# Raw parameters loaded in 2 KB runs, thirty-five copies placed on the other engine, one subtraction for two in a linear-attention and state-space kernel

## The chip, the cores and the metric

The kernel runs on one core of one Trainium2 chip. The core has TensorE (PE, matmuls into PSUM), VectorE (DVE), ScalarE (ACT), GpSimd (POOL, here only fills and DMA issues) and SyncE (SP, DMA issues). Each engine executes its own instructions in order; semaphores order the engines among each other. The metric is the device time of one execution in microseconds (us), as the median of several runs. The trace was taken from one further, profiled execution.

## What is computed

Two independent branches on 2048 tokens of width 448, whose bf16 results are put side by side into 896 columns. Branch A is linear attention with 16 heads of 28 and the feature map softmax(p), softmax(-p); branch B is a state-space convolution with 448 channels of 256 complex states each.

```python
# A
q, k, v = split(x @ wqkv)                       # 16 heads of 28
phi = lambda p: concat(softmax(p), softmax(-p))
phi_q, phi_k = phi(q @ w_phi), phi(k @ w_phi)
kv = einsum("bhsf,bhsd->bhfd", phi_k, v);  z = phi_k.sum(tokens)
o  = (phi_q @ kv) / (phi_q @ z + 1e-6)
a  = o @ wo
# B
dt = exp(log_dt);  P = exp(dt * (A_re + 1j*A_im) * l)        # l = 0..2047
K  = einsum("dn,dnl,dn->dl", C, P, dt*B).real
y  = irfft(rfft(u, 4096) * rfft(K, 4096))[:2048] + u * Dskip
out = concatenate([a, y], axis=-1)
```

## The kernel before

The program is recorded first: each call of a helper adds one operation to a list (`Prog.add`), some 1100 in all, and names its engine. Then the operations are issued in the order of a table of numbers, `ORDER`, written out by hand; a second table, `SLOTS`, names the PSUM bank of each job. So the order of instructions on each engine is that of the table, and the waits between engines follow from which operation reads or overwrites what. PSUM has eight banks; a bank that ScalarE and VectorE both read is read by one after the other.

The helpers are `mul`, `add`, `sub` (VectorE, line 162), `smul` (VectorE, times a constant, L174), `vcopy` (VectorE, L180), `recip` (VectorE, L187), `af` (ScalarE function, L190), `acopy` (copy on ScalarE, L193), `mms` and `transposes` (TensorE, L201 and L211), `dma` (L216, from SP or POOL). A copy that changes f32 to bf16 is named CAST in the trace.

The stages, by the names of the functions:

- Raw parameters: six arrays of 448x256 bf16 (A, B, C, real and imaginary) are loaded, 224 KB each. `to_states` multiplies them by diagonal matrices DG of dt, which also brings states to the partitions: 128 states (two halves of 256) by 896 columns of channels. `log_dt` is loaded as [4, 112], put through exp and turned on TensorE into [112, 4] in PSUM. For A, ScalarE copies the result from PSUM to bf16 (the high part), and VectorE subtracts that from PSUM (the low part); ScalarE exponentials read the same banks. From A come powers (`amp`, `cs`, PW) by products, from B and C the coefficients CR. `ones` matmuls over CR give K0.
- `flip_x` transposes x on TensorE; a copy brings it back to SBUF. `fold_weights` multiplies the key and query weights with w_phi. `signal_spectrum(b)`, b = 0, 1: sums and differences of u, matmuls with a table G1, and eight copies of 128x896 from PSUM, then a store to SUd in DRAM.
- `key_side`: eight pairs of token blocks. For a pair: projections on TensorE, four exponentials and two copies of V on ScalarE, one DMA transpose by SP (L600) into the one buffer ET, 14 matmuls of ET with a constant HZ (the sums of the softmax), a reciprocal on VectorE (L187), a product VR on VectorE, 16 matmuls that add to the key-value sums. HZ lies in SBUF where `ones` lay before.
- For a quarter `qt` of the channels: `rotations` and `dampings` (sines and exponentials on ScalarE), `damp`, `far`, `hi_tables` (products on VectorE, the largest 128x6720), `build_k` (small matmuls and copies), `scatter_k` (through DRAM), then kernel spectrum and `conv` (products of 3584, sums, inverse matmuls, store). `query_side(sc)`, sc = 0 to 3, stands between them.

The operations of the four quarters, the two signals, the pairs of keys and the query blocks are interleaved by ORDER.

Of the kernel before, what the change touches and what calls it, by code (L numbers as in the profile page):

```python
# [46 lines left out]
def _dft_tables():  # L47
# [6 lines left out]
    GI = np.stack([GO, GO[:, :, :, ::-1]])  # L54
    e = _round_bf16(np.arange(2048)).astype(np.int64)
# [27 lines left out]
class Prog:  # L83
# [10 lines left out]
    def add(self, eng, fn):  # L94
        self.ops.append((eng, fn))

    def issue(self, i):
        self.ops[i][1]()
# [7 lines left out]
def kernel(  # L106
# [57 lines left out]
    def mul(o, a, b):  # L164
        tt(o, a, b, ALU.mult)
# [4 lines left out]
    def sub(o, a, b):  # L170
        tt(o, a, b, ALU.subtract)

    def smul(o, a, s):
        prog.add("V", lambda: nc.vector.tensor_scalar_mul(o, a, s))  # L174
# [4 lines left out]
    def vcopy(o, a):  # L179
        prog.add("V", lambda: nc.vector.tensor_copy(o, a))  # L180
# [11 lines left out]
    def acopy(o, a):  # L192
        prog.add("A", lambda: nc.scalar.copy(o, a))  # L193
# [60 lines left out]
    ldt = sb(oSQ + 2816, [4, 112])  # L254
    dtr = sb(oSQ + 3072, [4, 112])

    def load_raw(nm):
        dma("S", raw[nm], srcs[nm].rearrange("(j p) n -> p j n", p=112))
# [5 lines left out]
    dma("S", ldt, bass.AP(tensor=B_log_dt.tensor, offset=B_log_dt.offset, ap=[[112, 4], [1, 112]]))  # L264
# [38 lines left out]
    (b_,) = prog.take("P", 6)  # L303
    dtp = bank16(b_, [112, 4])
    transposes([(dtp, dtr, PID[0:4, 0, 0:4])])
    mul(DG, PID[0:112, 0, 0:112].unsqueeze(1).to_broadcast([112, 4, 112]), dtp.unsqueeze(2).to_broadcast([112, 4, 112]))
# [38 lines left out]
    for part, terms in enumerate(([("CreBre", DG), ("CimBim", DGN)], [("CreBim", DG), ("CimBre", DG)])):  # L345
# [141 lines left out]
    def damp(qt, x0, w):  # L487
        A = amps(qt)
        smul(W[:, 1, 0:31:2, x0:x0 + w], A[:, 0:31:2, x0:x0 + w], -1.0)
        for part in (1, 0):  # L490
            for r, n, d, tr in ((0, 15, QC, 0), (30, 1, 0, 15)):
                o = W[:, part, r, x0:x0 + 1]
                a, step = A[:, r, x0:x0 + 1], d
                if part:
                    step = A[:, r + d // QC, x0:x0 + 1].offset - o.offset
                    a = o
                b = T[:, part, tr, x0:x0 + 1]
                if n > 1:
                    mul(view(o, [2 * QC, n], [d, 2], [1, w]), view(a, [2 * QC, n], [step, 2], [1, w]),
                        view(b, [QC, n], [0, 2], [1, w]))  # L500
                else:
                    mul(view(o, [1, w]), view(a, [1, w]), view(b, [1, w]))
# [53 lines left out]
    def build_k(qt, c):  # L556
        for hq in range(2):
# [12 lines left out]
            x0 = 14 * c + 7 * hq  # L570
            acopy(TS[qt % 2][:, :, x0:x0 + 7], psum[:, b, 0:7 * N_LO].rearrange("p (c l) -> p l c", c=7))
# [178 lines left out]
    def conv(qt, SU, UD, S_, OB, banks):  # L750
# [7 lines left out]
        def finish(b, t):  # L758
# [5 lines left out]
            sub(S[:, 1, 0], y[:, 0, 0:448], y[:, 0, 448:896])  # L764
            sub(S[:, 1, 1], y[:, 1, 448:896], y[:, 1, 0:448])
# [156 lines left out]
```

## Time and profile before

| | |
|---|---|
| median of 3 runs | 302.82 us (300.65 to 304.51) |
| profiled execution | 301.71 us, span 299.6 us |
| granted TensorE clock, mean | 0.949 |
| busy: TensorE, VectorE, ScalarE, POOL | 240.7, 244.4, 203.4, 16.0 us |
| VectorE idle before its last key reciprocal (114.89 us) | 40.6 us |
| VectorE idle from there to its last instruction (292.90 us) | 8.0 us |

The span runs from the first to the last instruction of the trace; the profiled execution's time is 2.1 us longer than it. "Busy" is time in which at least one instruction of the engine runs; instructions overlap a little in the pipeline, so that the sum of their durations is somewhat larger. A wait is put down to what released it.

### The profile page before, as it was taken

To read this page: it belongs to the slowest core of one execution; us is meant where nothing else is said; L and a number is where in the kernel's file an instruction comes from. 1 tells how busy PE (TensorE), PEld (TensorE's weight loads), DVE (VectorE), ACT (ScalarE), POOL (GpSimd) and SP (SyncE) were. 2 spreads that over 40 slices of the span, in tenths; PEclk is the share of its full clock that TensorE was granted. 3 is DMA by queue.
4 is the path that set the end of the run, shared out by engine and by line. 5 is a ranking of instruction groups with operands and counts; after the bars stand their busy time and mean duration, and the time that the engine had idled before them with its cause. 6 is when DMAs were issued, how large, how long until landed. Compare 5 with 4: busy or idle time off the path is not lost. (4 is left out here: it accounts for less than half of the span.)

```text
span 299.6 us, 8829 instructions
## 1 busy us (share of the span) xinstructions
PE 240.7 (80%) x3877; PEld 179.8 (60%) x3877; DVE 244.4 (82%) x292; ACT 203.4 (68%) x343; POOL 16.0 (5%) x32
## 2 busy tenths in 40 slices
PE   1246997899469999986979996566998888999784
PEld 1245554567245567863447763466658678999784
DVE  4265995446249999997989999989899999999991
ACT  3749999599947999997199955871948611544431
POOL 8102201001000000000000001000000000000000
PEclk9999999999959999998695999777999999999999
DMA  7999387463804530045012533955879956667222
GB/s 161 239 231 194 79 246 145 64 181 67 107 10 122 122 64 4 6 136 104 3 61 58 85 79 85 331 146 109 227 255 293 301 136 176 147 184 135 46 65 63
DMA packets 65966, 39.47 MB, mean 132 GB/s; under 512 B 46616, under 2 KB 61992, under 8 KB 65544
## 3 DMA queue, kind: packets, MB, share of 16 engines
q1 hardware_dynamic: 62920, 31.57, 45.0%
q0 software_dynamic: 3008, 7.34, 8.9%
q8 instruction: 30, 0.49, 0.7%
q14 instruction: 8, 0.07, 0.1%
HBM read 26.36 MB, written 8.85 MB: 118 GB/s over the span
## 5 line engine op out<-in xcount | busy, mean ns | idle before, releaser
L201 PE MATMUL psum<-sbuf 128*16 128x48 bf16 (+9 forms) x3768 | 231.3, 258 | 39.1 <-DVE sbuf L162 11.1
L201 PEld LDWEIGHTS <-sbuf 128*16 128x16 bf16 (+4 forms) x3768 | 170.7, 109 | 98.3 <-issue 37.3
L162 DVE TENSOR_TENSOR sbuf<-sbuf 128x896 bf16<-128x896 bf16 (+13 forms) x227 | 216.7, 1002 | 12.1 <-DMA sbuf<-SCd 3.5
L193 ACT CAST sbuf<-psum 128x448 bf16<-128x448 f32 (+4 forms) x141 | 74.9, 581 | 70.6 <-PE psum L201 63.1
L190 ACT ACTIVATE sbuf<-psum 128x448 bf16<-128x448 f32 (+4 forms) x140 | 81.7, 674 | 13.2 <-DVE sbuf L162 7.5
L211 PE MATMUL psum<-sbuf 128*112 128x128 bf16 (+3 forms) x109 | 11.7, 267 | 16.2 <-DMA sbuf<-in_A_x_dram 7.2
L190 ACT ACTIVATE sbuf<-psum,sbuf 128x896 bf16<-128x896 f32 (+3 forms) x28 | 21.7, 812 | 0.0
L211 PEld LDWEIGHTS <-sbuf 128*112 128x112 bf16 (+3 forms) x109 | 10.0, 172 | 17.8 <-DMA sbuf<-in_A_x_dram 7.7
L187 DVE RECIPROCAL sbuf<-psum 128x64 bf16<-128x64 f32 x8 | 4.4, 555 | 19.4 <-PE psum L201 19.4
L190 ACT ACT_TABLE_LOAD x13 | 16.7, 1283 | 0.9 <-PEq L906 0.7
L190 ACT ACTIVATE sbuf<-sbuf 128x896 bf16<-128x896 bf16 (+3 forms) x13 | 11.6, 915 | 3.6 <-DVE sbuf L162 3.4
L180 DVE COPY sbuf<-psum 112x1024 bf16<-112x1024 bf16 (+2 forms) x16 | 7.3, 466 | 7.8 <-PE psum L211 6.6
L216 POOL DMA_DIRECT2D sbuf<-const x4 | 2.2, 556 | 126.0 <-PE psum L201 109.5
L162 DVE TENSOR_TENSOR sbuf<-psum,sbuf 128x128 f32<-128x128 f32 (+3 forms) x10 | 4.7, 491 | 3.8 <-ACT sbuf L193 3.8
L193 ACT COPY sbuf<-psum 112x896 bf16<-112x896 bf16 x5 | 4.5, 919 | 4.7 <-PE psum L211 4.7
L216 POOL DMA_DIRECT2D sbuf<-in_B_u_dram x8 | 6.6, 830 | 19.0 <-DMA sbuf<-in_B_B_re_dram 18.9
L174 DVE TENSOR_SCALAR sbuf<-sbuf 128x3584 bf16<-128x3584 bf16 (+4 forms) x11 | 6.5, 587 | 0.0
L216 POOL DMA_DIRECT2D sbuf<-SUd x4 | 2.1, 529 | 72.5 <-DVE sbuf L162 72.5
L193 ACT CAST sbuf<-sbuf 128x1792 bf16<-128x1792 f32 x3 | 5.1, 1703 | 0.0
L180 DVE COPY sbuf<-sbuf 128x448 bf16<-128x448 bf16 (+1 forms) x6 | 1.4, 238 | 3.1 <-DMA sbuf<-const 3.1
L177 DVE SCALAR_TENSOR_TENSOR sbuf<-sbuf 128x64 f32<-128x64 f32 (+1 forms) x6 | 3.0, 506 | 0.0
L196 POOL MEMSET sbuf<- 128x32 bf16 (+3 forms) x6 | 1.4, 261 | 24.7 <-PE psum L211 24.5
(12 smaller groups left out, 9.4 us busy)
## 6 DMA issues: line engine op xcount, KB each, us to landing
sbuf<-const SPq DMA_DIRECT2D x16, 384.0 KB, 3.2
SUd<-sbuf SPq DMA_DIRECT2D x8, 448.0 KB, 4.3
sbuf<-SCd SPq DMA_DIRECT2D x16, 224.0 KB
sbuf<-SUd POOLq DMA_DIRECT2D x4, 896.0 KB, 4.9
sbuf<-const POOLq DMA_DIRECT2D x2, 1024.0 KB, 7.9
sbuf<-in_A_x_dram SPq DMA_DIRECT2D x4, 448.0 KB
out_dram<-sbuf SPq DMA_DIRECT2D x4, 448.0 KB
sbuf<-in_B_u_dram SPq DMA_DIRECT2D x16, 112.0 KB, 4.0
```

The lines of the kernel that those rows point to most:

```text
L162: prog.add("V", lambda: nc.vector.tensor_tensor(out=o, in0=a, in1=b, op=op))
L174: prog.add("V", lambda: nc.vector.tensor_scalar_mul(o, a, s))
L177: prog.add("V", lambda: nc.vector.scalar_tensor_tensor(out=o, in0=a, scalar=s, in1=b, op0=op0, op1=op1))
L180: prog.add("V", lambda: nc.vector.tensor_copy(o, a))
L187: prog.add("V", lambda: low(lambda: nc.vector.reciprocal(o, a)))
L190: prog.add("A", lambda: nc.scalar.activation(o, a, fn, **kw))
L193: prog.add("A", lambda: nc.scalar.copy(o, a))
L196: prog.add("G", lambda: nc.gpsimd.memset(o, v))
L201: nc.tensor.matmul(o, lhsT=l, rhs=r, **kw)
L211: nc.tensor.transpose(o, i, idn)
L216: prog.add(eng, lambda: e.dma_start(out=o, in_=i))
```

## The change

1. Raw parameters are loaded as "(p j) n" instead of "(j p) n": partition p holds channels 4p to 4p+3, one run of 2 KB, instead of four runs of 512 B from channels p, 112+p and so on. `log_dt` comes as [112, 4] in the same manner, so that its transpose on TensorE, and the bank for it, fall away. The order of columns that the later stages expect is restored in `to_states`, whose matmuls have 56 columns instead of 112 and are twice as many (48 to 96), in the K0 matmuls (8 to 16), and in the column steps of the copy to TS in `build_k`.
2. `Prog.add` takes a second form of an operation, for the other engine. 35 operations, listed in OTHER, are issued in that form. 18 go from ScalarE to VectorE: nine copies of 128x896 f32 from PSUM (the high part of A, real and imaginary, one half of CR, six of signal_spectrum), one of 112x896 f32 and three of 112x896 bf16 in fold_weights, three of 448 columns f32 from PSUM (K0, one V of keys, one of the query side), two casts of 128x1792 f32 in SBUF (two powers). 17 go from VectorE to ScalarE: two copies of flip_x, two tiny ones for KVZ, four of 128x128 f32 and four of 128x128 bf16 in query_side, two of 448 in hi_tables(2) and (3), and three multiplications by a constant (one of 3584 in damp(2), two of 448 in far(3)).
3. In `conv`, the two subtractions of 448 become one of 896; the sign goes into the table GI.
4. `damp` writes its parts in another order; the count and size of its operations stay.
5. ORDER and SLOTS are new.

```diff
+    GI[1, :, 1] *= -1
...
-    def add(self, eng, fn):
-        self.ops.append((eng, fn))
+    def add(self, eng, fn, other=None):
+        self.ops.append((eng, fn, other))
 
     def issue(self, i):
-        self.ops[i][1]()
+        eng, fn, other = self.ops[i]
+        (other if i in OTHER else fn)()
...
     def smul(o, a, s):
-        prog.add("V", lambda: nc.vector.tensor_scalar_mul(o, a, s))
+        prog.add("V", lambda: nc.vector.tensor_scalar_mul(o, a, s), lambda: nc.scalar.activation(o, a, ACT.Copy, scale=s))
...
     def vcopy(o, a):
-        prog.add("V", lambda: nc.vector.tensor_copy(o, a))
+        prog.add("V", lambda: nc.vector.tensor_copy(o, a), lambda: nc.scalar.copy(o, a))
...
     def acopy(o, a):
-        prog.add("A", lambda: nc.scalar.copy(o, a))
+        prog.add("A", lambda: nc.scalar.copy(o, a), lambda: nc.vector.tensor_copy(o, a))
...
     def load_raw(nm):
-        dma("S", raw[nm], srcs[nm].rearrange("(j p) n -> p j n", p=112))
+        dma("S", raw[nm], srcs[nm].rearrange("(p j) n -> p j n", j=4))
...
-    dma("S", ldt, bass.AP(tensor=B_log_dt.tensor, offset=B_log_dt.offset, ap=[[112, 4], [1, 112]]))
+    dma("S", ldt, bass.AP(tensor=B_log_dt.tensor, offset=B_log_dt.offset, ap=[[4, 112], [1, 4]]))
...
     af(dtr, ldt, ACT.Exp)
-    (b_,) = prog.take("P", 6)
-    dtp = bank16(b_, [112, 4])
-    transposes([(dtp, dtr, PID[0:4, 0, 0:4])])
-    mul(DG, PID[0:112, 0, 0:112].unsqueeze(1).to_broadcast([112, 4, 112]), dtp.unsqueeze(2).to_broadcast([112, 4, 112]))
+    mul(DG, PID[0:112, 0, 0:112].unsqueeze(1).to_broadcast([112, 4, 112]), dtr.unsqueeze(2).to_broadcast([112, 4, 112]))
...
         for j in range(4):
             for nch in range(2):
-                at = (j % 2) * QC + nch * 56
-                o = view(psum[:, bs[j // 2], at:at + 1], [112, 2], [14, 4], [1, 14])
-                items += acc(o, [(t[:, j, 128 * nch:128 * nch + 128],
-                                  d[:, j, :].rearrange("p (g c q) -> p c g q", c=2, q=14)) for t, d in terms])
+                for h in range(2):
+                    at = 112 * (j // 2) + 56 * nch + 7 * (j % 2)
+                    o = view(psum[:, bs[h], at:at + 1], [QC, 2], [14, 4], [1, 7])
+                    items += acc(o, [(t[:, j, 128 * nch:128 * nch + 128],
+                                      d[:, j, 56 * h:56 * h + 56].rearrange("p (a g r) -> p a g r", a=2, r=7))
+                                     for t, d in terms])
...
             add(S[:, 0], y[:, :, 0:448], y[:, :, 448:896])
-            sub(S[:, 1, 0], y[:, 0, 0:448], y[:, 0, 448:896])
-            sub(S[:, 1, 1], y[:, 1, 448:896], y[:, 1, 0:448])
+            sub(S[:, 1], y[:, :, 0:448], y[:, :, 448:896])
...
+OTHER = {int(i) for i in (
+    "33 36 49 52 56 73 94 98 102 104 110 112 115 130 132 152 155 157 232 330 333 445 453 499 507 588 625 633 644 "
+    "666 674 706 768 902 936 "
+).split()}
```

Three places show how the new order moves instructions. Lines of the changed kernel are numbered two or three higher (L164 for L162, L195 for L193, L189 for L187).

VectorE, from the start, after its three fills. Before, the first four operations are DG, the low part of A's real part, DGN and a copy of flip_x:

```order
L162 TENSOR_TENSOR sbuf<-sbuf,psum 112x448
L162 TENSOR_TENSOR sbuf<-psum,sbuf 128x896
L174 TENSOR_SCALAR sbuf<-sbuf 112x448
L180 COPY sbuf<-psum 112x2x4x128
L180 COPY sbuf<-sbuf 112x16
L180 COPY sbuf<-psum 112x2x4x128 x2
```

Now, with the copies of the high parts (CAST 128x896) and the three bf16 copies of fold_weights (COPY 112x896) between them:

```order
L164 TENSOR_TENSOR sbuf<-sbuf 112x448
L176 TENSOR_SCALAR sbuf<-sbuf 112x448
L195 CAST sbuf<-psum 128x896
L164 TENSOR_TENSOR sbuf<-psum,sbuf 128x896
L195 CAST sbuf<-psum 128x896
L164 TENSOR_TENSOR sbuf<-psum,sbuf 128x896
L164 TENSOR_TENSOR sbuf<-sbuf 112x1024 x4
L164 TENSOR_TENSOR sbuf<-sbuf 128x1792
L182 COPY sbuf<-psum 112x2x4x128
L164 TENSOR_TENSOR sbuf<-sbuf 128x1792
L195 COPY sbuf<-psum 112x896
L182 COPY sbuf<-psum 112x2x4x128
```

Both pairs of copy and subtraction are on VectorE, and the four products of raw parameters (112x1024) follow directly.

VectorE, in the key stage. Before, from the fifth reciprocal to behind the sixth; the products of 6720 are damp(0), those of 3584 and 2x1792 far(0):

```order
L187 RECIPROCAL sbuf<-psum 128x64
L162 TENSOR_TENSOR sbuf<-sbuf 128x1856
L174 TENSOR_SCALAR sbuf<-sbuf 128x16x224
L162 TENSOR_TENSOR sbuf<-sbuf 128x6720
L162 TENSOR_TENSOR sbuf<-sbuf 128x224
L162 TENSOR_TENSOR sbuf<-sbuf 128x6720
L162 TENSOR_TENSOR sbuf<-sbuf 128x224
L162 TENSOR_TENSOR sbuf<-sbuf 128x2x1792
L162 TENSOR_TENSOR sbuf<-sbuf 128x3584
L162 TENSOR_TENSOR sbuf<-sbuf 128x1792
L187 RECIPROCAL sbuf<-psum 128x64
```

Now, from the second reciprocal to the fourth:

```order
L189 RECIPROCAL sbuf<-psum 128x64
L164 TENSOR_TENSOR sbuf<-sbuf 128x1856
L164 TENSOR_TENSOR sbuf<-sbuf 128x3584
L164 TENSOR_TENSOR sbuf<-sbuf 128x4x224
L164 TENSOR_TENSOR sbuf<-sbuf 128x224
L164 TENSOR_TENSOR sbuf<-sbuf 128x4x224
L164 TENSOR_TENSOR sbuf<-sbuf 128x6720
L189 RECIPROCAL sbuf<-psum 128x64
L164 TENSOR_TENSOR sbuf<-sbuf 128x1856
L164 TENSOR_TENSOR sbuf<-sbuf 128x3584
L164 TENSOR_TENSOR sbuf<-sbuf 128x6720
L189 RECIPROCAL sbuf<-psum 128x64
```

The two products of 6720 stand in two different gaps between reciprocals, three pairs earlier.

ScalarE, between the powers of A and the copies of the first signal. Before, the big exponential (128x1792) is followed by copies of fold_weights and of the signal (128x2x4x112), and by the sines of A:

```order
L190 ACTIVATE sbuf<-sbuf 128x1792
L193 CAST sbuf<-psum 112x896
L190 ACTIVATE sbuf<-psum,sbuf 128x896
L190 ACTIVATE sbuf<-psum 128x896
L193 CAST sbuf<-psum 112x896
L190 ACTIVATE sbuf<-psum,sbuf 128x896
L193 CAST sbuf<-sbuf 128x1792
L193 CAST sbuf<-psum 128x2x4x112 x2
```

Now, from the same operation on; the functions on 128x224 and 128x2x224, and those of 128x896 after them, are rotations(0):

```order
L192 ACTIVATE sbuf<-sbuf 128x1792
L195 CAST sbuf<-psum 128x896
L192 ACTIVATE sbuf<-psum 128x896
L192 ACTIVATE sbuf<-psum,sbuf 128x224
L192 ACTIVATE sbuf<-psum 128x224
L195 CAST sbuf<-psum 112x896
L192 ACTIVATE sbuf<-psum 128x2x224
L192 ACTIVATE sbuf<-psum,sbuf 128x896
L195 CAST sbuf<-psum 112x896
L192 ACTIVATE sbuf<-psum 128x224
```

The cast of a power and the signal's copies have left this place, and rotations(0) fill it; before, these stood behind the fifth pair's exponentials.

## Rows read from the trace of the kernel before

**Rows 1.** The page, part 1: busy us (share of the span) and instructions
```profile
PE 240.7 (80%) x3877; PEld 179.8 (60%) x3877; DVE 244.4 (82%) x292; ACT 203.4 (68%) x343; POOL 16.0 (5%) x32
```

**Rows 2.** Windows: length, busy of each engine, clock, DMA share, GB/s
```profile
0.00:10.00 10.00, 1.15 (x9) 0.85 (x9) 4.07 (x6) 4.10 (x5) 7.17 (x15) 1.00 0.80 190
10.00:53.88 43.88, 30.72 (x240) 20.59 (x241) 29.15 (x37) 37.23 (x48) 4.45 (x8) 1.00 0.81 178
53.88:114.89 61.01, 53.38 (x478) 33.89 (x480) 41.12 (x41) 51.80 (x85) 1.25 (x3) 0.94 0.46 91
114.89:292.90 178.01, 152.29 (x3096) 121.48 (x3097) 170.04 (x212) 109.23 (x204) 3.18 (x6) 0.93 0.50 134
292.90:299.60 6.70, 3.13 (x64) 2.97 (x61) 0.00 (x0) 1.06 (x2) 0.00 (x0) 1.00 0.31 67
```

**Rows 3.** VectorE's longest wait: us in total, times, longest
```profile
DVE sbuf L187 <- PE psum L201: 19.4, 5, 8.4
```

**Rows 4.** VectorE's timeline: start, us, line, operation, [idle before <-releaser]
```profile
53.88 0.56 DVE L187 RECIPROCAL sbuf<-psum 128x64 bf16<-128x64 f32 x1 [4.70 <-PE psum L201]
...
74.53 0.55 DVE L187 RECIPROCAL sbuf<-psum 128x64 bf16<-128x64 f32 x1
...
85.22 0.56 DVE L187 RECIPROCAL sbuf<-psum 128x64 bf16<-128x64 f32 x1 [8.38 <-PE psum L201]
...
89.12 12.79 DVE L162 TENSOR_TENSOR sbuf<-sbuf 128x6720 bf16<-128x6720 bf16 x7
101.83 0.55 DVE L187 RECIPROCAL sbuf<-psum 128x64 bf16<-128x64 f32 x1
...
114.89 0.56 DVE L187 RECIPROCAL sbuf<-psum 128x64 bf16<-128x64 f32 x1 [0.43 <-PE psum L201]
```

**Rows 5.** VectorE's groups by form: busy us, mean ns of one, idle before
```profile
L162 DVE TENSOR_TENSOR sbuf<-sbuf 128x896 bf16<-128x896 bf16 x58 | 34.6, 619 | 0.9
...
L162 DVE TENSOR_TENSOR sbuf<-sbuf 128x448 bf16<-128x448 bf16 x32 | 11.3, 384 | 0.2
...
L162 DVE TENSOR_TENSOR sbuf<-sbuf 128x1792 bf16<-128x1792 f32 x3 | 6.0, 2015 | 0.0
L180 DVE COPY sbuf<-psum 112x1024 bf16<-112x1024 bf16 x8 | 5.3, 678 | 6.0 <-PE psum L211 6.0
...
L174 DVE TENSOR_SCALAR sbuf<-sbuf 128x3584 bf16<-128x3584 bf16 x3 | 3.3, 1085 | 0.0
...
L162 DVE TENSOR_TENSOR sbuf<-psum,sbuf 128x896 bf16<-128x896 f32 x2 | 2.2, 1087 | 3.8 <-ACT sbuf L193 3.8
...
L162 DVE TENSOR_TENSOR sbuf<-psum,sbuf 112x448 bf16<-112x448 f32 x2 | 1.2, 620 | 0.0
...
L180 DVE COPY sbuf<-psum 128x128 f32<-128x128 f32 x4 | 1.1, 287 | 1.2 <-PE psum L201 1.1
```

**Rows 6.** ScalarE's groups by form, the large copy from PSUM
```profile
L193 ACT CAST sbuf<-psum 128x896 bf16<-128x896 f32 x20 | 18.2, 934 | 7.7 <-PE psum L201 7.5
```

**Rows 7.** Timeline, columns as in rows 4: HZ on POOL, its matmuls, wo, the fifth pair
```profile
48.01 0.58 POOL L216 DMA_DIRECT2D sbuf<-const  x1 [16.53 <-issue]
...
53.27 2.90 PE L201 MATMUL psum<-sbuf 128*128 128x32 bf16 x26 [2.90 <-DMA sbuf<-const]
...
74.38 0.75 POOL L216 DMA_DIRECT2D sbuf<-in_A_wo_dram  x1 [0.15 <-issue]
...
84.62 7.37 PE L201 MATMUL psum<-sbuf 128*128 128x32 bf16 x50 [3.26 <-DMA sbuf<-sbuf]
```

**Rows 8.** Timeline, columns as in rows 4: the matmuls behind VectorE's last operation
```profile
292.32 3.71 PE L201 MATMUL psum<-sbuf 128*128 128x112 bf16 x72 [1.04 <-DVE sbuf L162]
```

More of the change, by code (lines that the diff above doesn't have):

```diff
@@ L253 @@
     DGN = sb(oSQ + 1920, [112, 4, 112])
-    ldt = sb(oSQ + 2816, [4, 112])
-    dtr = sb(oSQ + 3072, [4, 112])
+    ldt = sb(oSQ + 2816, [112, 4])
+    dtr = sb(oSQ + 2824, [112, 4])
     def load_raw(nm):
-        dma("S", raw[nm], srcs[nm].rearrange("(j p) n -> p j n", p=112))
+        dma("S", raw[nm], srcs[nm].rearrange("(p j) n -> p j n", j=4))
     def load_x(i):
@@ L351 @@
     bs = prog.take("P", 0)
-    mms([it for qt in range(4) for it in acc(
-        view(psum[:, bs[0], 112 * qt:112 * qt + 1], [28, 4], [14, 2], [1, 14]),
-        [(ones, view(CR[:, 0, QC * qt + 56 * nch:QC * qt + 56 * nch + 1], [14, 4], [112, 2], [1, 14]))
+    mms([it for qt in range(4) for c in range(2) for it in acc(
+        view(psum[:, bs[0], 112 * qt + 2 * c:112 * qt + 2 * c + 1], [28, 4], [1, 2], [4, 7]),
+        [(ones, view(CR[:, 0, QC * qt + 112 * c + 56 * nch:QC * qt + 112 * c + 56 * nch + 1], [14, 4], [7, 2], [1, 7]))
          for nch in range(2)])])
@@ L488, in damp, with rows_of @@
         A = amps(qt)
[L489 to L502, printed above, removed]
+        inside = qt in (0, 3)
+        def rows_of(part, a, step):
+            mul(view(W[:, part, 0, x0:x0 + 1], [2 * QC, 15], [QC, 2], [1, w]),
+                view(a[:, 0, x0:x0 + 1], [2 * QC, 15], [step, 2], [1, w]),
+                view(T[:, part, 0, x0:x0 + 1], [QC, 15], [0, 2], [1, w]))
+            mul(W[:, part, 30, x0:x0 + w], a[:, 30, x0:x0 + w], T[:, part, 15, x0:x0 + w])
+        if not inside:
+            rows_of(0, A, QC)
+        N_ = W[:, 1] if inside else A
+        smul(N_[:, 0:31:2, x0:x0 + w], A[:, 0:31:2, x0:x0 + w], -1.0)
+        rows_of(1, N_, QC - WS if inside else QC)
+        if inside:
+            rows_of(0, A, QC)
     def tmp(i):
@@ L569, in build_k @@
                 mms(items)
-            x0 = 14 * c + 7 * hq
-            acopy(TS[qt % 2][:, :, x0:x0 + 7], psum[:, b, 0:7 * N_LO].rearrange("p (c l) -> p l c", c=7))
+            acopy(TS[qt % 2][:, :, 2 * c + hq:28:4], psum[:, b, 0:7 * N_LO].rearrange("p (c l) -> p l c", c=7))
     def scatter_k(qt):
```

92 rows, old and new, of tables (ORDER, SLOTS) are left out of this document.

## Prediction, made before the changed kernel was run

> **What bounds the kernel now.** I read the page's busy shares first. VectorE is busy for 244.4 us of the 299.6, TensorE for 240.7, ScalarE for 203.4 [rows 1]. Two engines at 80% or more, each waiting for the other in turn: the averages don't say which sets the end, so the stretches come next.
>
> The windows cut the run at the first and the last of the eight reciprocals of the key stage [rows 2]. From the last one (114.89) to VectorE's last instruction (292.90) VectorE is busy 170.04 of 178.01 us: 8.0 idle. This stretch is as long as VectorE's work in it. Before 114.89 VectorE is busy 4.07 + 29.15 + 41.12 = 74.3 us, so it idles 40.6. Behind 292.90 comes a tail of 6.7 us: 72 matmuls in 3.71 us [rows 8], an eviction, a store.
>
> So the end is: time of the last key reciprocal + VectorE's work behind it + 8.0 + tail. Work taken from VectorE late is worth its full length. Work given to VectorE early is free as long as it falls into the 40.6 us.
>
> What makes the 40.6? The waits put 19.4 us of it to reciprocals that wait for TensorE, the longest 8.4 [rows 3]. In VectorE's timeline the reciprocals start at 53.88, three steps later at 74.53 (6.9 us a step), then at 85.22, 101.83 and, two steps later, 114.89 [rows 4]. Three places lose time. The first reciprocal: TensorE sits 2.90 us until 53.27 for a constant, HZ, whose load POOL issued only at 48.01 [rows 7]. HZ lies where the matrix `ones` was, so it waits for the K0 matmuls, which stand late. The fifth: TensorE waits 3.26 us for a DMA transpose, beside which ran the load of `wo`, issued at 74.38 [rows 7]. That step took 10.7 us, 3.8 over the 6.9. The sixth: 12.79 us of VectorE in one piece from 89.12, damp(0) and what follows it, stand ahead of the reciprocal at 101.83 [rows 4].
>
> **VectorE's sum.** 18 copies come from ScalarE. Ten read 128x896 or 112x896 f32 from PSUM. No copy of that form stands on VectorE; the nearest row is the subtraction with one such operand, 1.087 [rows 5]. Neighbours overlap a little in the pipeline, so I take 1.05: 10.5 us. The lower bound is the bf16 copy of 112x1024, 0.678, cut to 896 elements: 0.6 each, 6 us. Three bf16 copies of 112x896 at 0.59: 1.8. Three of 448 f32 from PSUM, nearest row 0.620 [rows 5], at 0.58: 1.7. Two casts of 1792 f32 in SBUF lie, by the nearest rows, between 0.678 (the bf16 copy) and 2.015 (a product of 1792 with an f32 operand) [rows 5]; the first is the less like it, so I take a little over the middle, 1.5: 3.0. Together 17.0, bounds 11 and 19.
>
> By the row for the same f32 copy on ScalarE, 0.934 [rows 6], the ten are about 1.2 us dearer on VectorE in all. The Trainium skill ("VectorE: DVE Perf Modes", Specifications) says the same in words, that ScalarE sits closer to PSUM. Its tier table and errata formula speak of the two SBUF casts: a one-source f32 operation may run at double rate there, an estimated 0.99 us each, by which the sum would be 1.0 lower; no row here shows it.
>
> 17 operations go to ScalarE: two flip copies at 0.678, one scaling of 3584 at 1.085, and fourteen small ones, none over the 0.287 of the 128x128 copy [rows 5], at 0.25: 5.9, less overlap 5.3. The convolution's two subtractions of 448 become one of 896, eight times: 8 x (2 x 0.384 - 0.619) = 1.2 [rows 5]. New sum: 244.4 + 17.0 - 5.3 - 1.2 = 254.9.
>
> Of the 18, only one copy of 448 (query side) stands behind the last key reciprocal; of the 17, the scaling and twelve small ones do (3.7 with overlap). Work behind it: 170.0 + 0.6 - 3.7 - 1.2 = 165.7. Work up to it: 254.9 - 165.7 = 89.2.
>
> **First reciprocal.** Ahead of it VectorE had 33.2 us. By the new order 13 of the copies come in ahead: seven f32 at 1.05, three at 0.59, one at 0.58, two at 1.5, 12.7 together. Steps of hi_tables(0) (about 2.0 by their forms), one flip copy and two tiny copies go behind it or away. That leaves 43. At the start VectorE still idles: the states of A_re wait for their load, and ScalarE's exponentials read the same banks. Before, it was busy 4.07 of the first 10 us [rows 2], some 6 idle; the second pair of banks now costs about 2 more: 8. So VectorE is there at 51. K0's copy now stands behind some 25 us of VectorE's work, and its matmuls ahead of that, so HZ's load goes out well before 48 and no longer holds TensorE. I take 51.
>
> **To the last reciprocal.** Seven steps, each the longer of 6.9 (transpose, matmuls, reciprocal, product, matmuls) and VectorE's work in it. The order now spreads damp(0) and far(0) over the steps; by the forms VectorE's work in them is 6.4, 8.6, 7.2, 5.8, 6.5, 6.8 and 5.1. That gives 8.6 + 7.2 + 5 x 6.9 = 50.3. It can be spread because the rotations of table 0, which stood on ScalarE between the exponentials of the fifth and the sixth pair, now stand ahead of all key exponentials. The load of `wo` still goes beside some transpose; between 0 and the 3.8 seen I take 1.5. Last reciprocal: 51 + 50.3 + 1.5 = 102.8, against 114.9. Idle up to there: 102.8 - 89.2 = 13.6 instead of 40.6.
>
> **End.** 102.8 + 165.7 + 8.0 = 276.5. Tail 6.7 less 0.5, since VectorE's last operation is now an addition and half of the 72 matmuls need only the subtraction ahead of it: 6.2. Span 282.7. The profiled run took 301.71 with a span of 299.6, so 2.1 lie around it: 284.8, which is 16.9 less. The median of the runs shown, 302.82, stands 1.1 above the profiled one; I forecast 285.
>
> **Costed at nothing.** The 2 KB runs for raw parameters: one load, A_re, stands on the way at the start; the others land while VectorE has other work. Bounds: 1 us gained there, or 1 lost, because x now follows all six raw loads. The 56 more matmuls (48 for the states, 8 for K0): TensorE did 240 in 30.72 us there [rows 2], 0.13 each, 7 together. It is busy 32 of the first 54 us, and this idle hides them; without it the first reciprocal would be up to 7 later. ScalarE loses about 17 and gains about 7; it idles 96 in all.
>
> **Rivals.** (1) The key loop keeps its pace. The loss would not lie in VectorE's order but in the one ET buffer, which a transpose may overwrite only when TensorE has read it, and in what TensorE does in between. Then 61.0 us pass from first to last reciprocal as before: from 51, 112.0 + 165.7 + 8.0 + 6.2 + 2.1 = 294.0; from 53.9, 296.9. For it: even with undisturbed transposes a step took 6.9, and VectorE waited. Against: the two long steps (10.7 and 16.6) have other causes with names, above.
>
> (2) Slower: in the first 51 us TensorE's banks are emptied by VectorE, in order. A copy that stands behind a 2-us product whose operand is late keeps its bank, and TensorE's next matmuls, those of the keys included, wait. To reach 308.9 (2% slower; about 2% is what a measurement of this kernel can tell from no change) the last reciprocal must come at 126.9, 24.1 later than forecast: 1.9 us lost for each of the 13 copies. Two each give 311. Against: ScalarE, which emptied these banks, was itself busy 37.23 of 43.88 us there, VectorE only 29.15 [rows 2].
>
> (3) Denser: VectorE hardly waits after the start. 8 + 89.2 = 97.2, then 165.7 + 3 + 6.2 + 2.1 = 274.2. The steps' sum of 50.3 speaks against it.
>
> (4) The placement doesn't do what it says: each copy moved to VectorE displaces VectorE's own work, and the idle stays at 40.6. 89.2 + 40.6 + 165.7 + 8.0 + 6.2 + 2.1 = 311.8. The waits would have to be set from outside both engines, as by the loads. Half of it (idle at 27) gives 298.
>
> **Chances.** Forecast 0.52 (279 to 290 for it alone); rival 1 0.25, two thirds of it under 296.8; denser 0.10; half of rival 4, 297 to 308, 0.08; rivals 2 and 4 whole 0.05. Faster by over 2%: 0.52 + 0.16 + 0.10 = 0.78; within 2%: 0.17; slower: 0.05. The range 276 to 298 leaves out half of the denser case, most of the half of rival 4 and the slower ones: 0.17.
>
> **What would show it.** VectorE's busy time near 255 and ScalarE's near 193; the first reciprocal near 51 and the last near 103; VectorE's idle before the last near 14; an f32 PSUM copy of 896 on VectorE near 1.05, the SBUF cast near 1.5; HZ issued well before 48. The forecast is wrong if the first reciprocal starts later than 54, or if the steps stay above 8 us: then look at whom TensorE waits for in the first 50 us, and at how long the transposes take.

## The result, and the profile after

The changed kernel took 287.74 us as the median of four runs (286.73 to 292.33), the kernel before 303.66 beside it. The ratio is 0.950, with an interval of 0.939 to 0.960. Two later comparisons with other runs of the kernel before gave 0.953 (0.944 to 0.963) and 0.951 (0.945 to 0.957). The forecast was 285 within 276 to 298. The profiled execution took 286.73 us with a span of 284.6, against 301.71 and 299.6 before.

The page's first part after the change (columns as in [rows 1]):

```profile
PE 236.7 (83%) x3932; PEld 179.9 (63%) x3932; DVE 255.6 (90%) x285; ACT 202.2 (71%) x340; POOL 16.1 (6%) x32
```

VectorE does 11.2 us more than before in a run that is 15 us shorter. The windows, cut at the first and the last key reciprocal and at VectorE's last instruction (columns as in [rows 2]):

```profile
0.00:10.00 10.00, 1.04 (x16) 0.88 (x16) 3.65 (x6) 5.18 (x7) 6.64 (x15) 1.00 0.82 176
10.00:52.32 42.32, 34.16 (x333) 24.84 (x334) 38.45 (x41) 34.87 (x47) 6.25 (x11) 1.00 0.73 175
52.32:99.03 46.71, 45.43 (x425) 28.64 (x423) 45.87 (x47) 40.52 (x73) 0.00 (x0) 1.00 0.55 121
99.03:277.70 178.67, 152.85 (x3101) 122.44 (x3100) 167.64 (x193) 120.61 (x214) 3.17 (x6) 0.95 0.51 136
277.70:284.60 6.90, 3.22 (x66) 3.06 (x63) 0.00 (x0) 1.06 (x2) 0.00 (x0) 1.00 0.29 63
```

Up to the last reciprocal VectorE is now busy 3.65 + 38.45 + 45.87 = 88.0 of 99.0 us: 11.1 idle where it was 40.6. Between the first and the last reciprocal it idles 0.8 us of 46.7, before 19.9 of 61.0. The last reciprocal comes 15.9 us earlier. Behind it the stretch is as long as before, 178.7 us: VectorE works 2.4 us less there, and idles 11.0 instead of 8.0. So the whole gain lies ahead of the last key reciprocal. TensorE has less to do between the two reciprocals as well: 425 matmuls and 45.4 us where it had 478 and 53.4 [rows 2]. It is recorded busy 97% of that stretch now, VectorE 98%.

VectorE's timeline at the reciprocals (start, us, line, operation, idle before where there was any; beside [rows 4]):

```profile
52.32 0.56 DVE L189 RECIPROCAL sbuf<-psum 128x64 bf16<-128x64 f32 x1
...
58.72 0.55 DVE L189 RECIPROCAL sbuf<-psum 128x64 bf16<-128x64 f32 x1
59.38 8.01 DVE L164 TENSOR_TENSOR sbuf<-sbuf 128x1856 bf16<-128x1856 bf16 x6
67.31 0.55 DVE L189 RECIPROCAL sbuf<-psum 128x64 bf16<-128x64 f32 x1
...
94.06 0.55 DVE L189 RECIPROCAL sbuf<-psum 128x64 bf16<-128x64 f32 x1
...
99.03 0.55 DVE L189 RECIPROCAL sbuf<-psum 128x64 bf16<-128x64 f32 x1
```

No reciprocal has a wait in brackets any more; the 19.4 us of [rows 3] are gone. The steps are 6.4, 8.6, 7.2, 5.9, 6.7, 6.9 and 5.0 us. The load of HZ goes out at 30.61 and that of `wo` at 50.97, ahead of the second transpose (issued at 52.30); a transpose is hardly waited for any more (0.2 us, once) (POOL's timeline):

```profile
30.61 0.57 POOL L218 DMA_DIRECT2D sbuf<-const  x1 [1.82 <-PE psum L203]
...
50.97 0.75 POOL L218 DMA_DIRECT2D sbuf<-in_A_wo_dram  x1 [0.29 <-ACT sbuf L192]
```

What the moved operations cost on their new engine (groups by form: busy us, mean ns of one, idle before):

```profile
L195 DVE CAST sbuf<-psum 128x896 bf16<-128x896 f32 x9 | 9.6, 1081 | 7.6 <-ACT sbuf L192 5.7 <-PE psum L203 1.9
...
L195 DVE CAST sbuf<-sbuf 128x1792 bf16<-128x1792 f32 x2 | 2.2, 1085 | 0.0
```

and on ScalarE, with the copies to TS of `build_k`, whose written columns the change spreads:

```profile
L195 ACT CAST sbuf<-psum 128x336 bf16<-128x336 f32 x16 | 14.3, 994 | 10.6 <-PE psum L203 10.6
...
L176 ACT ACTIVATE sbuf<-sbuf 128x3584 bf16<-128x3584 bf16 x1 | 3.2, 3190 | 0.1
...
L182 ACT COPY sbuf<-psum 112x1024 bf16<-112x1024 bf16 x2 | 2.1, 1044 | 0.0
```

### The profile page after: what moved, and what is told of

It reads as the page before. It is cut to its first block, busy times and chain, and to the rows that moved or that the text cites. A ratio compares the mean times of both kernels' runs of the same rounds, so it can differ in the third digit from the quotient of the medians.

```text
span 284.6 us, 8940 instructions
## 1 busy us (share of the span) xinstructions
PE 236.7 (83%) x3932; PEld 179.9 (63%) x3932; DVE 255.6 (90%) x285; ACT 202.2 (71%) x340; POOL 16.1 (6%) x32
## 4 chain that ended last, share of the span: by engine, by line
DVE 36%; PE 32%; DMA 15%; issue 7%; ACT 5%; SPq 3%; POOL 1%; DVEq 0%; POOLq 0%
DVE sbuf L164 33%; PE psum L203 31%; DMA sbuf<-SCd 7%; DMA sbuf<-in_A_x_dram 5%; ACT sbuf L192 3%; SPq L218 3%; ACT sbuf L195 2%; DMA SCd<-sbuf 1%; DVE sbuf L189 1%; DVE sbuf L176 1%; DMA out_dram<-sbuf 1%; DMA sbuf<-in_B_u_dram 1%; PE psum L213 1%; POOL sbuf L218 1%; ACT L192 0%
## 5 line engine op out<-in xcount | busy, mean ns | idle before, releaser
L203 PE MATMUL psum<-sbuf 128*16 128x48 bf16 (+10 forms) x3824 | 229.0, 256 | 36.0 <-DVE sbuf L164 10.5
L164 DVE TENSOR_TENSOR sbuf<-sbuf 128x896 bf16<-128x896 bf16 (+13 forms) x220 | 217.2, 1033 | 10.4 <-PE psum L203 3.5
L195 ACT CAST sbuf<-psum 128x448 bf16<-128x448 f32 (+4 forms) x128 | 70.9, 605 | 55.7 <-PE psum L203 54.1
L192 ACT ACTIVATE sbuf<-psum 128x448 bf16<-128x448 f32 (+4 forms) x140 | 83.9, 668 | 9.9 <-PE psum L203 9.7
L195 DVE CAST sbuf<-psum 128x896 bf16<-128x896 f32 (+2 forms) x13 | 12.4, 974 | 7.7 <-ACT sbuf L192 5.7
L213 PE MATMUL psum<-sbuf 128*112 128x128 bf16 (+2 forms) x108 | 10.3, 259 | 8.2 <-DVE sbuf L164 7.0
L213 PEld LDWEIGHTS <-sbuf 128*112 128x112 bf16 (+2 forms) x108 | 9.1, 165 | 9.8 <-DMA sbuf<-in_A_x_dram 5.5
L192 ACT ACTIVATE sbuf<-sbuf 128x896 bf16<-128x896 bf16 (+3 forms) x13 | 11.8, 905 | 4.6 <-DVE sbuf L164 3.9
L176 DVE TENSOR_SCALAR sbuf<-sbuf 128x896 bf16<-128x896 bf16 (+3 forms) x8 | 4.9, 609 | 1.7 <-ACT sbuf L192 1.5
L182 ACT COPY sbuf<-psum 128x128 f32<-128x128 f32 (+2 forms) x10 | 4.3, 427 | 2.6 <-PE psum L213 2.1
L164 DVE TENSOR_TENSOR sbuf<-psum,sbuf 128x128 f32<-128x128 f32 (+3 forms) x10 | 4.7, 492 | 0.5 <-ACT sbuf L182 0.4
L176 ACT ACTIVATE sbuf<-sbuf 128x448 bf16<-128x448 bf16 (+1 forms) x3 | 4.4, 1455 | 0.9 <-DVE sbuf L164 0.9
L189 DVE RECIPROCAL sbuf<-psum 128x64 bf16<-128x64 f32 x8 | 4.4, 550 | 0.1
L182 DVE COPY sbuf<-psum 112x1024 bf16<-112x1024 bf16 x6 | 4.1, 684 | 0.3 <-PE psum L213 0.2
```

What stands on the lines that cost most here:

```text
L164: prog.add("V", lambda: nc.vector.tensor_tensor(out=o, in0=a, in1=b, op=op))
L176: prog.add("V", lambda: nc.vector.tensor_scalar_mul(o, a, s), lambda: nc.scalar.activation(o, a, ACT.Copy, scale=s))
L182: prog.add("V", lambda: nc.vector.tensor_copy(o, a), lambda: nc.scalar.copy(o, a))
L189: prog.add("V", lambda: low(lambda: nc.vector.reciprocal(o, a)))
L192: prog.add("A", lambda: nc.scalar.activation(o, a, fn, **kw))
L195: prog.add("A", lambda: nc.scalar.copy(o, a), lambda: nc.vector.tensor_copy(o, a))
```

## Experiments

All ratios are to the kernel before on the same chip. The changed kernel itself ran again beside HZ, wo and the four copies (0.953, 286.52 us), and beside the second run of the raw parameters, the TS copies and the two operations (0.951, 285.49 us). The other runs are compared with it by these ratios.

A time in a trace can differ between executions. In the six traces whose operations ahead of the first reciprocal are those of the changed kernel, that reciprocal starts between 51.90 and 54.00 us.

**The order without the placement.** The changed kernel, all 35 operations on their old engines:

```diff
-OTHER = {33, 36, 49, 52, 56, 73, ... 936}
+OTHER = set()
```

> The changed kernel with all 35 operations back on their old engines; order, banks and loads of the changed kernel stay. Theory (the end is the last key reciprocal plus VectorE's work behind it, and the placement fills VectorE's idle time of the first 50 us while ScalarE is relieved there): VectorE's work behind the last reciprocal grows by about 3.1 us, and ScalarE, busy 40 of the first 52 us, takes 13 copies of 0.6 to 1.7 us back, 12 us, so that it sets the pace there: first reciprocal at 57 to 60 instead of 52.3, time 295 to 299. Rival (the new order alone carries the gain, the placement only swaps one busy engine for another): first reciprocal within 1 us of 52.3, time 290 to 292.

304.16 us, 1.014 of the kernel before (1.0005 to 1.028). The four times were 300.36, 303.24, 305.08 and once 658.53 us, which no trace explains and which lifts the median; so no gain is shown, rather than a loss. The theory's side, but dearer than I had it. Its windows (columns as in [rows 2]; the execution of 300.36 us), from start to first and from first to last reciprocal:

```profile
0.00:60.12 60.12, 36.62 (x353) 25.90 (x354) 31.89 (x35) 49.97 (x64) 12.84 (x26) 1.00 0.65 152
60.12:107.06 46.94, 44.72 (x420) 28.11 (x418) 42.64 (x46) 40.87 (x72) 0.08 (x1) 1.00 0.55 120
```

ScalarE works 50.0 of the first 60.1 us, and VectorE waits for it:

```profile
DVE sbuf L164 <- ACT sbuf L195: 20.9, 3, 12.9
```

20.9 us on three copies, the longest 12.9. So the placement moved the first reciprocal from 60.1 to 52.3. The seven steps behind it take 46.9 us without it and 46.7 with it: they are the order's. The last key reciprocal thus comes 7.8 us earlier by the new order and loads (114.89 to 107.06) and 8.0 more by the placement (99.03). Yet the order alone is no gain: behind the last reciprocal 191.1 us pass, 6.4 more than in the kernel before and 5.6 more than in the changed kernel. Against the changed kernel VectorE has 2.9 us more work there, about what the theory had, and idles 2.6 us more.

**The placement without the order.** The kernel before with the three helpers' second forms and the same 35 operations in OTHER, by their numbers there:

```diff
-    def acopy(o, a):
-        prog.add("A", lambda: nc.scalar.copy(o, a))
+    def acopy(o, a):
+        prog.add("A", lambda: nc.scalar.copy(o, a), lambda: nc.vector.tensor_copy(o, a))
...
+OTHER = {34, 37, 50, 53, 57, 74, ... 939}
```

> The kernel before, in its own order, banks and loads, with the same 35 operations on the other engine. Theory (placement needs the order that fits it): VectorE's early work grows by 15 us inside an order whose key stage idled for other reasons (HZ late, wo beside a transpose, damp(0) in one piece), so that the last key reciprocal stays between 112 and 118; behind it VectorE has 4 us less: 297 to 303. Rival (placement alone is the gain): last reciprocal at 105 or earlier, time 288 to 293.

325.08 us, 1.083 (1.074 to 1.093): worse than any expectation. The waits of VectorE (us in total, times, longest):

```profile
DVE sbuf L188 <- PE psum L202: 14.3, 4, 8.4
DVE sbuf L163 <- ACT sbuf L191: 13.2, 4, 7.3
DVE sbuf L194 <- ACT sbuf L191: 9.3, 2, 6.1
DVE sbuf L163 <- ACT sbuf L175: 5.3, 2, 3.8
```

The reciprocals still wait 14.3 us (19.4 before). New are waits of the moved operations and of those behind them. The copies at the start stand on VectorE where ScalarE's functions still hold the banks (L194 <- L191, 9.3). Behind the last reciprocal, at 119.1, the run takes 204.4 us instead of 184.7, with VectorE idle some 30 us: two scalings of 448 (L175) and other functions come late on ScalarE. ScalarE itself had stood 9.81 us there, by the profile for a store. Its timeline, and VectorE's:

```profile
244.53 2.09 ACT L194 CAST sbuf<-psum 128x448 bf16<-128x448 f32 x5 [9.81 <-DMA out_dram<-sbuf]
...
249.62 0.69 DVE L163 TENSOR_TENSOR sbuf<-sbuf 128x448 bf16<-128x448 bf16 x2 [7.33 <-ACT sbuf L191]
251.81 1.89 DVE L163 TENSOR_TENSOR sbuf<-sbuf 128x896 bf16<-128x896 bf16 x4 [1.49 <-ACT sbuf L175]
...
258.20 3.83 DVE L163 TENSOR_TENSOR sbuf<-sbuf 128x896 bf16<-128x896 bf16 x5 [3.77 <-ACT sbuf L175]
```

This is the way rival 4 would have gone, and it needs only that a moved operation stands in a place that its new engine reaches late.

**Only the moves to VectorE.** The changed kernel with 17 fewer operations in OTHER:

```diff
-OTHER = {33, 36, 49, 52, 56, 73, 94, 98, ... 936}
+OTHER = {33, 36, 49, 52, 56, 73, 102, 104, 110, 112, 115, 130, 132, 152, 155, 157, 232, 644}
```

> The changed kernel with the 18 copies on VectorE as changed, but the 17 operations that went to ScalarE back on VectorE. Theory (VectorE's work is the length of the run from the first reciprocal on): 5.3 us more of VectorE's work, 3.7 of it behind the last key reciprocal, all of it on the path: last reciprocal about 1 later, time 291.5 to 293.5. Rival (VectorE's late work has slack against TensorE and ScalarE, idle 11 us there): under 290.

293.15 us, 0.973 (0.961 to 0.985). VectorE is busy 260.4 us, 4.8 more than the changed kernel; the span of the profiled run is 290.8, 6.2 more. As the theory says, the work shows in the time, though the intervals of the two ratios just touch. Five waits for TensorE at the 128x128 copies are new (5.5 us, the longest 3.25); the changed kernel's wait of 3.5 us at 247 is gone.

**HZ.** The kernel before with one address changed:

```diff
-    ones = sb(186944, [128, 128])
+    ones = sb(205504, [128, 128])
```

> The kernel before with one address changed: the matrix ones stands at 205504 and no longer where HZ comes to lie, so HZ's load need not wait for the K0 matmuls. Theory (HZ cost TensorE 2.9 us ahead of the first reciprocal): HZ's load is issued near 32 instead of 48, the first reciprocal comes at 50.5 to 51.5, the next three 2 to 3 earlier as well, and the time falls by 2 to 3 us unless a later step takes it back. Rival (the transpose and its matmuls weren't ready either): the first reciprocal stays within 0.7 of 53.9 and the time the same.

298.25 us, 0.990 (0.985 to 0.996): 2.9 us faster. POOL and VectorE:

```profile
31.13 0.61 POOL L216 DMA_DIRECT2D sbuf<-const  x1
```

```profile
52.18 0.56 DVE L187 RECIPROCAL sbuf<-psum 128x64 bf16<-128x64 f32 x1 [1.16 <-PE psum L201]
```

HZ goes out at 31.1, and the first reciprocal comes 1.7 earlier, not 2.9: TensorE's other work then ends last. The last one comes at 112.78, 2.1 earlier. The 2.9 us are by the ratio.

**wo.** The kernel before, with number 162 (the load of `wo`) in ORDER right behind 161 (that of Dskip):

```diff
-... 282 161 284 345 ... 332 162 363 ...
+... 282 161 162 284 345 ... 332 363 ...
```

> The kernel before with one operation earlier in its order: the load of wo stands right behind that of Dskip on POOL and is issued near 49 instead of 74, when no transpose is under way. Theory (that load slowed the fifth transpose to 8 us): the fifth reciprocal comes 3.5 to 4.5 earlier (81 to 82), the transpose takes 2.3 to 2.9 us like the others, the last reciprocal comes 3 to 4 earlier, and so does the end: 3 to 4 us faster. Rival (the fifth transpose was slow for another reason, or the pair behind it takes the gain back, since VectorE's 12.8 us of damp(0) stand behind it): fifth reciprocal as before, or the time the same within 1 us.

299.34 us, 0.995 (0.990 to 1.0001): by the ratio 1.5 us faster, but the interval reaches 1, so that a gain in the time isn't shown. Its timelines:

```profile
50.55 0.75 POOL L216 DMA_DIRECT2D sbuf<-in_A_wo_dram  x1
```

```profile
82.32 0.56 DVE L187 RECIPROCAL sbuf<-psum 128x64 bf16<-128x64 f32 x1 [4.91 <-PE psum L201]
...
112.30 0.55 DVE L187 RECIPROCAL sbuf<-psum 128x64 bf16<-128x64 f32 x1
```

The step to the fifth reciprocal takes 7.2 us (75.10 to 82.32) instead of 10.7, so `wo` was what slowed that transpose. The next step takes part of it back (17.5 us instead of 16.6), as the rival had it; the last reciprocal is 2.6 earlier. If the effects of HZ and `wo` add, they make 4.7 of the 15.9 us that the last reciprocal gained in the changed kernel. How the rest divides, no run shows beyond the 7.8 and 8.0 above.

**Four copies back.** The changed kernel with 152, 155, 157 and 232 (three copies of signal_spectrum(1), one V) on ScalarE again:

```diff
-OTHER = {33, ... 132, 152, 155, 157, 232, 330, ...}
+OTHER = {33, ... 132, 330, ...}
```

> The changed kernel with four of the 18 copies back on ScalarE: the three of signal_spectrum(1) and the one of V, 3.6 us of VectorE's work within the key steps. Theory (a step is as long as VectorE's work in it; transposes and TensorE have room): the first, sixth and seventh step become shorter by 0.6, 1 and 2 us, the last reciprocal comes at 95.5 to 96.5 and the time falls by 2.5 to 3.5 against the changed kernel on this chip. Rival (another loop, of transposes, TensorE and ScalarE, stands close behind, near the 5 us of the shortest step, and ScalarE takes 3.4 us more): last reciprocal within 1 of 99, time the same or up to 2 us slower.

288.34 us, 0.961 (0.954 to 0.968): no gain. The first reciprocal stands at 54.00 here, 1.7 later, though none of the four copies lies ahead of it. The steps are 6.4, 8.6, 7.2, 5.9, 6.7, 7.0 and 5.6 us: the first six are as long as before. The copy of V lay in the first step, and all three others in the seventh, none in the sixth. The windows of these two steps (columns as in [rows 2]), here and then in the changed kernel:

```profile
54.00:60.40 6.40, 6.40 (x73) 4.67 (x72) 5.69 (x9) 6.40 (x14) 0.00 (x0) 1.00 1.06 265
95.74:101.32 5.58, 4.48 (x48) 2.83 (x47) 2.21 (x4) 5.58 (x10) 0.00 (x0) 1.00 0.53 72
```

```profile
52.32:58.72 6.40, 6.40 (x75) 4.59 (x73) 6.21 (x10) 6.16 (x13) 0.00 (x0) 1.00 1.08 264
94.06:99.03 4.97, 4.90 (x49) 3.05 (x48) 4.97 (x7) 4.97 (x10) 0.00 (x0) 1.00 0.59 81
```

The last reciprocal in VectorE's timeline:

```profile
101.32 0.56 DVE L189 RECIPROCAL sbuf<-psum 128x64 bf16<-128x64 f32 x1 [3.33 <-PE psum L203]
```

With 2.8 us less of VectorE's work in the seventh step, the last reciprocal waits 3.33 us for TensorE, and the step is 5.6 us instead of 5.0; ScalarE, which has the three copies again, is busy all of it. The first step keeps its length with 0.5 us less of VectorE's work: TensorE and ScalarE are busy all of it. So the rival holds for these two steps, in which other engines are as full as VectorE. In the other five nothing was moved, and no run shows whether VectorE's work alone sets their length.

**The changed kernel again**, as the measure for the runs beside it:

> The changed kernel once more, on the chip of the runs beside it, so that they can be compared with it: the same ratio to the kernel before as at first, 0.94 to 0.96. Any theory expects the first key reciprocal near 52.3 and the last near 99.0.

286.52 us, 0.953 (0.944 to 0.963); reciprocals from 52.62 to 99.32.

> The changed kernel again, as the measure for the three runs beside it. Any theory expects a ratio to the kernel before of 0.945 to 0.957, the first key reciprocal near 52.5 and the last near 99.2.

285.49 us, 0.951 (0.945 to 0.957).

**Raw parameters as before.** The changed kernel with the old loads, `log_dt` turned on TensorE, the old state and K0 matmuls and the old TS copies; the loads and the TS copies are shown:

```diff
-        dma("S", raw[nm], srcs[nm].rearrange("(p j) n -> p j n", j=4))
+        dma("S", raw[nm], srcs[nm].rearrange("(j p) n -> p j n", p=112))
...
-            acopy(TS[qt % 2][:, :, 2 * c + hq:28:4], psum[:, b, 0:7 * N_LO].rearrange("p (c l) -> p l c", c=7))
+            x0 = 14 * c + 7 * hq
+            acopy(TS[qt % 2][:, :, x0:x0 + 7], psum[:, b, 0:7 * N_LO].rearrange("p (c l) -> p l c", c=7))
```

> The changed kernel with the raw parameters and log_dt loaded as before (512-byte runs, log_dt turned on TensorE), the state matmuls of 112 columns and the contiguous copies to TS in build_k; order, banks and placement as changed. Theory (the loads are hidden): time within 1.5 us of the changed kernel's, the TS copies on ScalarE back at 0.55 from 0.99 us, ScalarE's busy time 6 to 7 lower without effect on the end. Rival A (2 KB runs bring the first parameters earlier, which is on the path at the start): 2 to 4 us slower, first reciprocal at 54 or later. Rival B (the slower TS copies delay the later stages): 2 us or more faster.

> Raw parameters, state matmuls and TS copies as before, the rest as changed, once more and beside the changed kernel itself, since the first comparison of the two (about 1.5% slower than the changed kernel) was within what the two intervals allow. Theory (2 KB runs are hidden; the second parameter lands 1.5 us later, and VectorE's queue makes it good before the first reciprocal): same as the changed kernel within 1 us, reciprocals within 0.5 us. Rival (2 KB runs are worth 2 to 4 us): slower by that, as it seemed.

291.10 us, 0.967 (0.955 to 0.979), and again 291.62, 0.970 (0.965 to 0.976): 2% slower than the changed kernel, 0.951 (0.945 to 0.957) beside the second run. The theory of "hidden, so the same" falls, and the rivals name the wrong place or the wrong sign. A's imaginary part does arrive later (VectorE's second copy at 14.69 and 15.62 instead of 13.22). The first and the last reciprocal stand at 52.53 and 99.24 in the first run, as in the changed kernel, and at 53.47 and 100.17 in the second, which is within what executions differ by. Behind the last reciprocal the two traces take 188.5 and 187.5 us, the changed kernel's 185.6 and, run again, 186.3. So the traces hold 1 to 3 us of the 6 by which the medians of the second run and of the changed kernel beside it differ. VectorE's longest wait of that stretch goes back to 190 us, to the small matmuls of `build_k`. TensorE's timeline of the second run there, and the same place of the changed kernel:

```profile
184.32 2.94 PE L203 MATMUL psum<-sbuf 128*16 128x48 bf16 x128 [0.22 <-issue]
188.05 2.95 PE L203 MATMUL psum<-sbuf 128*16 128x48 bf16 x128 [0.79 <-issue]
195.06 5.36 PE L203 MATMUL psum<-sbuf 128*16 128x48 bf16 x61 [4.07 <-issue]
```

```profile
188.28 3.97 PE L203 MATMUL psum<-sbuf 128*16 128x48 bf16 x113 [0.58 <-issue]
```

Three times TensorE stands with nothing in the profile to wait for, 128 matmuls apart, which are 256 instructions with their weight loads; the third time it stands 4.07 us. The changed kernel stands at this place too, 0.58 us in the trace shown and 1.90 run again. VectorE, behind it, waits 4.85 us at 201; in the changed kernel's two traces it waits 1.54 and 3.16 there. So the longer stand goes with 1.7 to 3.3 us more of VectorE's waiting. TensorE's granted clock differs as well: behind the 4.07 us it is 0.50, the level of 1.2 GHz, from 194 to 200, in the changed kernel's trace only from 197 to 200. What the clock adds is not told apart here. All waits of TensorE of this kind, in the second run and in the changed kernel (us, times, longest):

```profile
PE psum L203 <- issue: 10.2, 7, 4.1
```

```profile
PE psum L203 <- issue: 3.0, 4, 1.3
```

Between 186 and 195 us the DMA queue of instructions delivers one packet, beside 1.31 MB of data:

```profile
q1 hardware_dynamic: 1112, 1.31, 67.4%
q8 instruction: 1, 0.02, 0.7%
```

The Trainium skill ("Runtime: NRT & Kernel Launch", Instruction fetch mechanics) says that an engine's instructions are refilled in blocks of 16 KiB, 256 instructions, and that crossing a block is mostly hidden. The count of 256 agrees with the rows; if these waits are such crossings, they are not hidden here. The kernel with raw parameters as before has 55 matmuls fewer ahead of this place, so that its blocks would end elsewhere. That the place of the blocks makes part of the 2% is what the traces suggest (the first run too has 4.07 at the same place and 11.8 in all). No run here moved the blocks alone, and this experiment undoes the loads, the matmuls and the TS copies together, so the cause stays open.

**TS copies together.** The changed kernel, with the copies to TS writing neighbouring columns, which puts the columns of the convolution's kernel in another order:

```diff
-            acopy(TS[qt % 2][:, :, 2 * c + hq:28:4], psum
+            acopy(TS[qt % 2][:, :, 14 * c + 7 * hq:14 * c + 7 * hq + 7], psum
```

> The changed kernel with the copies to TS in build_k writing seven neighbouring columns, as before, and no longer every fourth: the columns then stand in another order than the later stages take them in, so the output is another; the amount of work is the same. Theory (the step of 8 bytes between the written elements made these 16 copies slower, 0.99 us for 0.53, and ScalarE has room for it): the copies take 0.52 to 0.55 us, ScalarE is busy 7 us less, the time is the same within 1 us. Rival (they delay the tables and so VectorE's later stages): 2 to 4 us faster than the changed kernel.

285.04 us, 0.942 (0.936 to 0.949), against 0.951 (0.945 to 0.957) beside it: 0.9% lower, with intervals that overlap, so that a gain isn't shown. ScalarE's copies:

```profile
L195 ACT CAST sbuf<-psum 128x336 bf16<-128x336 f32 x16 | 7.8, 535 | 11.5 <-PE psum L203 11.5
```

The step of 8 bytes between written elements is what makes the copies 0.99 us. Whether it costs the end anything isn't shown: VectorE's wait near 247 us for TensorE (3.5 in the changed kernel) is 0.2 in this run, but it is gone in the next experiment too, where the copies are spread.

**Two operations back.** The changed kernel with the scaling of 3584 (706) and a query-side copy (644) on their old engines:

```diff
-OTHER = {33, ... 633, 644, 666, 674, 706, 768, ...}
+OTHER = {33, ... 633, 666, 674, 768, ...}
```

> The changed kernel with two operations back on the engines of before: the scaling of 3584 in damp(2), which took 3.19 us on ScalarE against 1.085 on VectorE, and the query-side copy of 448, which has VectorE wait for the bank in some runs. Theory (VectorE's work behind the last reciprocal sets the end, but VectorE also waits 1.5 to 4.7 us for ScalarE near 200 us): VectorE's work grows by 0.5 us, that wait shrinks by 1 to 3: the same to 2 us faster than the changed kernel. Rival (VectorE's work alone counts): 0.5 to 1 us slower.

288.28 us, 0.959 (0.952 to 0.965): 0.8% higher, intervals overlapping. The wait near 200 us stays, 3.47 in this run, so the slow scaling wasn't its cause. It speaks for the rival, weakly. Of the variants that compute the same, none was faster than the changed kernel.

## Why the prediction was right, step by step

- **What bounds.** Right: last key reciprocal + VectorE's work behind it + its idle there + tail. 99.03 + 167.64 + 11.03 + 6.90 = 284.60. That VectorE's late work is on the path is what the run with only the moves to VectorE bears out.
- **VectorE's sum.** 254.9 forecast, 255.6 measured. The PSUM copies took 1.081 (1.05 taken), the copies of 448 0.617, the bf16 copies 0.616. The SBUF casts took 1.085, not 1.5: the estimate of 0.99 by the Trainium skill ("VectorE: DVE Perf Modes", the tier table and the errata formula) was nearer than a value between two rows of other operations.
- **First reciprocal.** 52.3 for 51: work 42.1 for 43, idle ahead of it 10.2 instead of 8. In the first 10 us it idles 6.3, as taken; behind them 3.9 where 2 were taken: 1.33 at the second copy, behind ScalarE's exponentials (TensorE had waited 4.05 for A's imaginary part), and 1.51 for TensorE at 27. The experiment without placement confirms what it rests on: without the 13 copies on VectorE, ScalarE sets it at 60.1.
- **Steps.** 46.7 for 50.3 + 1.5. VectorE's work in the seven steps, as summed by the forms, is within 0.2 us of the length that each step has now. Wrong was the floor of 6.9 us a step. It was read from steps in which VectorE waited, and taken for the pace of the loop. But TensorE was recorded busy nearly all through those three steps (windows of the kernel before, columns as in [rows 2]):

```profile
53.88:60.49 6.61, 6.61 (x63) 4.04 (x62) 3.46 (x4) 4.06 (x7) 0.00 (x0) 1.00 0.54 72
60.49:67.88 7.39, 7.12 (x67) 4.33 (x66) 3.30 (x5) 7.10 (x14) 0.00 (x0) 1.00 0.72 186
67.88:74.53 6.65, 6.27 (x76) 4.82 (x75) 4.26 (x4) 6.51 (x10) 0.66 (x3) 1.00 0.38 73
```

  ScalarE was, too, through two of them. So the 6.9 us held work that the old order gave these engines there, and were not the pace of the loop. With another order steps of 5.0 and 5.9 us occur. How short a step could get is not shown. `wo` cost nothing, since it went out ahead of the second transpose.
- **Behind the last reciprocal.** Work 167.6 for 165.7, idle 11.0 for 8.0: 5.0 us too little. The largest single waits are 3.5 for TensorE at 247 and 2.0 for a DMA at 119.
- **Tail.** 6.9 for 6.2. The half-microsecond was no gain: before, the two subtractions stood last, and half of the 72 matmuls needed only the addition ahead of them, as [rows 8] shows (they start at 292.32, ahead of VectorE's end at 292.90). Now they start at 277.21, ahead of its end at 277.70.
- **ScalarE.** 202.2 for 193, the largest miss. The 17 operations cost about 10 us there instead of 7: the scaling of 3584 takes 3.19 us for 1.085 on VectorE, a flip copy 1.04 for 0.68. And the TS copies, which I had left out of the costing, take 7 us more (0.994 for 0.549). What this cost the end isn't shown; the run with the TS copies together was no clear gain.
- **2 KB runs and small matmuls costed at nothing.** Right for the reciprocals, wrong for the end: undoing them together with the TS copies costs 2%. Part of it stands at 190 us in the traces; the rest and the cause are open.

The misses were -3.8 (last reciprocal), +5.0 (behind it) and +0.7 (tail). That they cancelled to 1.9 us of span is luck: the mechanism was right, but two terms were off by more than the sum. Rival 1 (the loop keeps its pace) is refuted by the steps. For the key stage alone rival 3 (denser) came nearer than the forecast: VectorE idles 0.8 us there. Rival 2 didn't occur: TensorE waited less than 1 us for the moved copies in the first 52 us. Its longest wait there, 5.3 us, ended at 16.67, when x had landed, which now follows the six raw loads. Rival 4 happened where the order didn't fit the placement.

## What to carry to other kernels

Find the engine that is busy all through the late part, and ask for each earlier stretch what keeps it idle: work moved onto it there is free, if the order brings it there when its input is ready and its bank free. Placement and order are one decision here: the order alone was no faster (1.014), the placement alone slower (1.083), both together 0.951. A step's length that was read while the engine waited is no floor for the step: see first which other engine was busy in it, and whether the order can put that work elsewhere.

## What I had not expected of the hardware

- TensorE can stand with nothing in the profile to wait for: after 128 small matmuls, 256 instructions, up to 4.07 us, with the data queues 67% busy. Over the runs here such waits sum to between 2.7 and 11.8 us; the two largest sums (10.2 and 11.8) are those of the kernel with the raw parameters as before. That it waits for its own instructions is not shown.
- On ScalarE a copy of 128x336 from PSUM took 0.53 us into neighbouring elements and 0.99 us with 8 bytes from one written element to the next.
- The same scaling of 128x3584 bf16 took 1.09 us on VectorE and 3.19 on ScalarE, while the f32 copy of 128x896 from PSUM took 1.08 and 0.93, and the bf16 copy of 112x1024 from PSUM 0.68 and 1.04.
